# Stage 3 units one step earlier, the second set at step 14, and denser weight units

## The chip, the cores and the metric

The kernel runs on one core of a Trainium2 chip. A core has a matrix engine (TensorE, PE in the profile, with its weight loads as PEld), a vector engine (VectorE, DVE), an engine for activations (ScalarE, ACT), a general engine (GpSimd, POOL) and a queue engine (SyncE, SP), which here only issues DMAs. Each engine runs its own instructions in program order and waits on semaphores for the others. The metric is the device time of one execution in microseconds, as the median of several runs.

## The reference

Two layers. The first is a long convolution by FFT over a sequence of 12480 positions, for 4 batches and 128 channels, whose filter comes from a small MLP; the second is a feed-forward network with a gated activation.

```python
h_filt = (np.maximum(pos_emb @ w1, 0.0) @ w2) * np.exp(-0.01 * pos)[:, None]
u = x * v
L = 2 * S
y = irfft(rfft(u, n=L, axis=1) * rfft(h_filt, n=L, axis=0), n=L, axis=1)[:, :S, :]
t = (x * y).reshape(B * S, D)          # 49920 tokens of 128 channels
h = t @ w_in                           # 128 -> 2048
g = h * (1.0 / (1.0 + np.exp(-1.702 * h)))
out = g @ w_out                        # 2048 -> 128
```

## The kernel before

The FFT is done as matrix products in three stages. Stage 1 transforms along 120 positions (26 units, one per pair of residues), stage 2 transforms along the 52 residues, multiplies the spectra and transforms back (31 units), and stage 3 transforms back along the 120 positions and multiplies by x. Between the stages the data goes through DRAM (`g_d`, then `z_d`). The sequence is cut into five sets (`SETS`: block of the sequence, batch, number of batches), and each set passes all three stages. The result of stage 3 is cut into 104 halves of 480 tokens; sets 0 and 1 give 13 halves each, sets 2 to 4 give 26 each.

**The opening.** The loop from line 678 runs set 0 through stages 1 and 2, one tick per unit: `pipe.tick(u)` advances every live unit by one piece (a unit is a generator and each `yield` ends a piece; `yield 1` only splits a piece), so that up to seven units overlap. After each tick `heat` puts matmuls on a zero tile into the PE queue, and `wpipe.tick` advances the weight units: the FFN weights come in as 64-bit floats, and each of the eight weight units (`weight_unit`, line 543) turns a quarter of one weight matrix into a high and a low part by twelve DVE instructions on 128x512 elements and one on ACT. `WHEN` (line 40) lists the ticks at which a unit begins; its first piece is the DMA, and two ticks later its arithmetic begins, in pieces of two DVE instructions. Stage 1 units begin at ticks 0 to 25, stage 2 units at ticks 31 to 61. The last 24 spectra of stage 2 (`KEEP`) stay in a pool on chip, `keep`.

**The handover.** Seven ticks from line 703 run stage 3 for half 0. After that comes the main loop (line 714): for each half `n` eight steps `k`, each with one `mm1` (six matmuls of 480 columns into a PSUM pair `h`, then two activations, `gh` and `gf`), the `lo` of the step before (`gl`, the rest that `gh` leaves, on DVE), and the `mm2` of three steps before (six matmuls into `acc`). `mm1` of half `n` reads `xh` and `xl` of its stage 3 unit. In step 1 and step 9 the kept spectra are stored to DRAM on POOL's queue; in step `HOLD` the pool `keep` is closed, the rows of `z_d` that no unit writes are filled with zeros on the same queue, and the pool `main` is opened in its place. A tile of `main` waits until what lay there has been read.

**The feed.** From step `HOLD` on, `feed.run(1.0)` puts one step's share of the convolution of sets 1 to 4 behind the FFN matmuls of the step. `conv_feed` gives the units with weights and a mark for each set; `feed.pace` sets the rate so that the mark is reached in a given number of steps, and `feed.reach` puts in what is left. `when(n)` is the step in which the stage 3 unit of half `n` begins, `begin` the list of these for the first half of each set.

**Stage 3** (`p3_unit`, line 484): four DMAs (`zt` twice, `vt`, `x3`) on POOL's queue, or SP's for the first two halves; three ticks later sixteen matmuls into a PSUM bank (line 520), `yq` on ACT and two adds on DVE; a tick later the product with x (line 536), a tick later `xh` on ACT, a tick later `xl` on DVE (line 541). In the kernel before, the unit of half `n + 1` begins in step 0 of half `n`. So its matmuls stand in step 3, its `xl` in step 6, and `mm1` reads it eight steps after its beginning. There are three buffers of `xh` and `xl`, two each of `zt`, `vt` and `x3`. The PSUM pool of these banks holds three, shared with the feed.

The output of a half is copied out of `acc` with the last `mm2` and stored in step 4 of the next half, on POOL's queue.

Of the kernel before, what the change touches and what calls it, by code (L numbers as in the profile page):

```python
# [28 lines left out]
NP = N2 // 2  # L29
# [6 lines left out]
STEPS = FC // 2  # L36
KEEP = 24
AHEAD = 2
HOLD = 11
WHEN = (2, 7, 12, 17, 22, 38, 45, 52)  # L40

PAIRS = [(n, N2 - n) for n in range(1, NP)] + [(0, NP)]
SETS = [(0, 0, 1), (0, 1, 1), (0, 2, 2), (1, 0, 2), (1, 2, 2)]
# [12 lines left out]
NH = len(HV)  # L56
# [59 lines left out]
def conv_ffn_kernel(  # L116
# [22 lines left out]
    def pool(name, bufs, **kw):  # L139
        return ctx.enter_context(tc.tile_pool(name=name, bufs=bufs, **kw))  # L140
# [24 lines left out]
    def sb(name, shape, dt, bufs, tag=None, where="s"):  # L165
        return ps[where].tile(shape, dt, tag=tag or name, bufs=bufs, name=name)

    def bank():
        return ps["p"].tile([128, 512], F32, tag="cv", name="cv")
# [373 lines left out]
    def weight_unit(src, dst, s, rw):  # L543
        ts, stt = nc.vector.tensor_scalar, nc.vector.scalar_tensor_tensor
        raw = sb("raw", [128, WCH, 2], U32, 2)
        nc.sync.dma_start(out=raw.rearrange(rw[0], **rw[1]), in_=src)
        yield
        yield
        lo, hi = raw[:, :, 0], raw[:, :, 1]
        r, b, e = (sb(f"w{i}", [128, WCH], U32, 1) for i in range(3))  # L550
        t, q = (sb(f"w{i}", [128, WCH], F32, 1) for i in range(3, 5))
        ts(out=r, in0=lo, scalar1=29, scalar2=None, op0=ALU.logical_shift_right)
        stt(out=b, in0=hi, scalar=3, in1=r, op0=ALU.logical_shift_left, op1=ALU.bitwise_or)
        yield
        ts(out=b, in0=b, scalar1=0x7FFFFFFF, scalar2=0x40000000, op0=ALU.bitwise_and, op1=ALU.bitwise_xor)
        stt(out=b, in0=hi, scalar=0x80000000, in1=b, op0=ALU.bitwise_and, op1=ALU.bitwise_or)
        yield
        ts(out=e, in0=hi, scalar1=20, scalar2=0x7FF, op0=ALU.logical_shift_right, op1=ALU.bitwise_and)
        stt(out=t, in0=e, scalar=897, in1=b.bitcast(F32), op0=ALU.is_ge, op1=ALU.mult)
        yield  # L560
        w_hi = dst[0][:, s]
        act(w_hi, t, ACTF.Copy)
        ts(out=r, in0=lo, scalar1=6, scalar2=0x7FFFFF, op0=ALU.logical_shift_right, op1=ALU.bitwise_and)
        ts(out=b, in0=t.bitcast(U32), scalar1=0xFF800000, scalar2=None, op0=ALU.bitwise_and)
        yield
        tt(out=r, in0=r, in1=b, op=ALU.bitwise_or)
        tt(out=q, in0=r.bitcast(F32), in1=b.bitcast(F32), op=ALU.subtract)
        yield
        tt(out=t, in0=t, in1=w_hi.bitcast(F32), op=ALU.subtract)
        stt(out=dst[1][:, s], in0=q, scalar=2.0 ** -23, in1=t, op0=ALU.mult, op1=ALU.add)  # L570

# [71 lines left out]
    def fill(o, q):  # L643
        d = z_d[o][:, KZ:KP].rearrange("r k (q c) -> r (k q) c", c=128)
        q.dma_start(out=d, in_=zero.unsqueeze(1).broadcast_to([128, d.shape[1], 128]))

    with tc.manual_schedule():
        keep_cm = tc.tile_pool(name="keep", bufs=1, side="right", reuse_waits="tile")
        with tc.tile_pool(name="ps0", bufs=3, space=PSUM) as ps0, tc.tile_pool(name="ps0b", bufs=1, space=PSUM) as ps0b, \
                tc.tile_pool(name="st", bufs=1) as st:  # L650
            p1_cm = tc.tile_pool(name="p1", bufs=1, side="right")
            ps["s"], ps["p1"] = st, p1_cm.__enter__()
            ps["p"] = type("P", (), {"tile": staticmethod(
                lambda shape, dt, tag, name: (ps0 if tag == "cv2" else ps0b).tile(shape, dt, tag=tag, name=name))})
            nc.vector.memset(zero, 0.0)
            nc.vector.memset(w1_sb, 0.0)
            nc.vector.memset(w2_sb, 0.0)
            nc.vector.memset(sgn_sb[0:64], 1.0)
            nc.vector.memset(sgn_sb[64:128], -1.0)
            p1_load(0)  # L660
            for h in range(2):
                nc.sync.dma_start(out=w1_sb[64 * h:64 * h + 64, 64 * h:64 * h + 64], in_=w1)
                nc.sync.dma_start(out=w2_sb[64 * h:64 * h + 64, h], in_=w2)
            nc.sync.dma_start(out=win_sb, in_=c_win)
            wb = ps0b.tile([128, 512], F32, tag="wb", name="wb")

            def heat(k):
                for _ in range(2 * k):
                    mm(out=wb[:, 0:256], lhsT=warm[:, 0:128], rhs=warm, start=True, stop=True)

            heat(32)
            pipe, wpipe = Pipe(), Pipe()
            wu = list(weight_units())
            for c in range(1, AHEAD):
                p1_load(c)
            units = [p1_start(p) for p in range(NP)] + [None] * 5
            units += [p2_start(v) for v in range(NV)] + [None] * 9
            for n, u in enumerate(units):
                if n == NP + 9:
                    p1_cm.__exit__(None, None, None)  # L680
                    ps["k"] = keep_cm.__enter__()
                pipe.tick(u)
                heat(1 if 4 < n < NP else 6 if NP < n < NP + 6 else 2)
                if n == 4:
                    nc.sync.dma_start(out=wf, in_=c_wf)
                    nc.sync.dma_start(out=wv, in_=c_wi)
                    fill(0, nc.sync)
                wpipe.tick(wu.pop(0) if n in WHEN else None)
            assert not wu and not wpipe.live and not pipe.live
            heat(36)  # L690
        ps["f"] = pool("ffn", 1, reuse_waits="tile")
        ps["p"] = pool("ps1", 3, space=PSUM, reuse_waits="tile")
        ps["h"] = pool("ps2", 2, space=PSUM)
        p3 = Pipe()

        def when(n):
            return (n - 1) * STEPS

        first = {next(i for i, hv in enumerate(HV) if hv[0] == o): o for o in range(1, 5)}
        begin = sorted(when(n) for n in first)  # L700
        feed = Feed(pipe, *conv_feed())
        feed.pace(0, begin[0] - HOLD)
        for n in range(7):
            p3.tick(p3_unit(0) if n == 0 else None)
            if n == 1:
                act(sgn0, zero[:, 0:1], ACTF.Gelu_apprx_sigmoid)
            if n == 3:
                b = bank()
                for _ in range(20):
                    mm(out=b[:, 0:256], lhsT=warm[:, 0:128], rhs=warm, start=True, stop=True)  # L710
        gate = shared["a3"]
        ffn = Ffn()
        pend = []
        for n in range(NH):
            for k in range(STEPS):
                if pend:
                    ffn.lo(pend[-1])
                if len(pend) == LAG - 1 and pend[0][1] == STEPS - 1:
                    ffn.mm2(pend.pop(0))
                pend.append(ffn.mm1(n, k))  # L720
                t = n * STEPS + k
                if t == 1:
                    nc.gpsimd.tensor_tensor(out=sgn0, in0=gate[:, 0:1], in1=gate[:, 0:1], op=ALU.mult)
                if t == 1 or t == 9:
                    for _ in range(KEEP // 2):
                        spec_store(*spectra.pop(0), nc.gpsimd)
                if t == HOLD:
                    keep_cm.__exit__(None, None, None)
                    for o in range(1, 5):
                        fill(o, nc.gpsimd)  # L730
                    ps["s"] = ctx.enter_context(tc.tile_pool(name="main", bufs=1, side="right", reuse_waits="tile"))
                if len(pend) == LAG:
                    ffn.mm2(pend.pop(0))
                if t >= HOLD:
                    feed.run(1.0)
                if n + 1 < NH:
                    new = None
                    if k == 0:
                        if n + 1 in first:
                            o = first[n + 1]  # L740
                            feed.reach()
                            if o < 4:
                                feed.pace(o, begin[o] - begin[o - 1] - 2)
                            else:
                                feed.rate = 0.0
                        new = p3_unit(n + 1)
                    p3.tick(new)
                if k == 4:
                    ffn.store()
        ffn.lo(pend[-1])  # L750
        for it in pend:
            ffn.mm2(it)
        ffn.store()
# [123 lines left out]
```

## Time and profile before

| what | us |
|---|---|
| median of 3 runs (lowest, highest) | 3096.07 (3087.53, 3098.12) |
| the profiled execution | 3093.0 |
| its span, first to last instruction | 3091.2 |
| PE, DVE, ACT, POOL busy in the span | 2991.3, 2150.2, 2085.6, 470.6 |
| first stage 2 matmul | at 107.5 |
| first matmul of the FFN | at 210.5 |

The profile is of one execution. A view of waits names the engine and line that waited, what ended the wait, the total, the count and the longest. A view of groups or of a timeline names line, engine, operation, the tile written and the tiles read; "x4" is a count. A view of stretches gives, for each, its length, the busy time of PE, PEld, DVE, ACT and POOL with their instruction counts, the granted clock of PE (1.00 is full), the mean busy share of the 16 DMA engines, and GB/s. Matmul ends are modelled, so neighbouring matmuls overlap a little in such sums.

### The profile page before, as it was taken

The numbers are of one execution on the slowest core, as the hardware profiler recorded it, in microseconds if no ns is written. First come the engines' busy times: TensorE is split into PE (matmuls) and PEld (weight loads), VectorE is DVE, ScalarE is ACT, GpSimd is POOL, SyncE is SP. The second block draws the span as 40 slices with busy tenths as digits, with TensorE's granted clock in tenths as the row PEclk, the third lists the DMA queues.
The fourth block names the chain that finished last, engine by engine and source line by source line (L and its number), as shares of the span: only waits on it lengthen the run. The fifth ranks groups of instructions, "written<-read, shape, count | busy, mean of one in ns | idle before, by whom it ended". The sixth has DMA issues, their size and how long they took to land.

```text
span 3091.2 us, 42465 instructions
## 1 busy us (share of the span) xinstructions
PE 2991.3 (97%) x15478; PEld 2351.4 (76%) x15478; DVE 2150.2 (70%) x2909; ACT 2085.6 (67%) x2689; POOL 470.6 (15%) x765
## 2 busy tenths in 40 slices
PE   8898999999999999999999999999999999999999
PEld 4357876688766688777778887777778888888888
DVE  6555677777777766999996558888895445444454
ACT  3455776688777677666667766666666777677676
POOL 1353111012100111101111111111111111111110
PEclk9898999999999999999999999999999999999999
DMA  9878998999777976655565425455442111111110
GB/s 283 275 267 260 259 281 268 287 307 310 252 251 243 279 203 209 194 185 189 190 193 153 135 64 164 155 171 168 155 159 69 47 59 46 45 60 45 58 46 27
DMA packets 261105, 541.88 MB, mean 175 GB/s; under 512 B 30978, under 2 KB 120762, under 8 KB 260898
## 3 DMA queue, kind: packets, MB, share of 16 engines
q1 hardware_dynamic: 205970, 377.29, 38.4%
q0 software_dynamic: 54928, 161.86, 17.5%
q8 instruction: 125, 2.05, 0.3%
q14 instruction: 82, 0.67, 0.1%
HBM read 330.24 MB, written 208.80 MB: 174 GB/s over the span
## 4 chain that ended last, share of the span: by engine, by line
issue 38%; PE 17%; DVE 7%; POOL 4%; DMA 1%; ACT 0%; SPq 0%; POOLq 0%; DVEq 0%
PE h L595 7%; PE acc L612 7%; DVE fgl L603 2%; POOL zt L494 2%; DVE t L423 1%; PE cv L520 1%; POOL out_dram L623 1%; POOL x L500 1%; DVE t L439 1%; DVE t L438 1%; POOL vt L498 1%; DVE t L443 1%; PE ab L330 1%; DVE t L441 1%; PE cv L178 1%
## 5 line engine op out<-in xcount | busy, mean ns | idle before, releaser
L603 DVE TENSOR_TENSOR fgl<-fg,fgh 128x960 fp32r<-128x960 f32 x832 | 956.6, 1153 | 496.5 <-ACT fg L597 494.3
L596 ACT ACTIVATE fgh<-h 128x960 fp32r<-128x960 f32 x832 | 810.1, 974 | 548.5 <-PE h L595 547.7
L595 PE MATMUL h<-xh,wi 128*128 128x480 f32 x3328 | 1143.7, 388 | 9.2 <-ACT fg L597 8.4
L612 PE MATMUL acc<-fgh,wo 128*128 128x480 f32 x3328 | 871.9, 384 | 0.0
L597 ACT ACTIVATE fg<-h 128x960 f32<-128x960 f32 x832 | 805.9, 969 | 20.5 <-DVE fgl L603 20.0
L595 PEld LDWEIGHTS h<-xh,wi 128*128 128x128 f32 x3328 | 630.5, 189 | 184.7 <-issue 38.1
L612 PEld LDWEIGHTS acc<-fgh,wo 128*128 128x128 f32 x3328 | 629.6, 190 | 111.6 <-issue 12.2
L595 PE MATMUL h<-xl,wi 128*128 128x480 f32 x1664 | 638.2, 384 | 36.3 <-DVE xl L541 36.3
L612 PE MATMUL acc<-fgl,wo 128*128 128x480 f32 x1664 | 503.2, 384 | 0.5 <-DVE fgl L603 0.4
L595 PEld LDWEIGHTS h<-xl,wi 128*128 128x128 f32 x1664 | 315.0, 189 | 91.7 <-DVE xl L541 47.2
L623 POOL DMA_DIRECT2D out_dram<-ot x104 | 57.1, 549 | 1990.4 <-ACT ot L616 1990.2
L612 PEld LDWEIGHTS acc<-fgl,wo 128*128 128x128 f32 x1664 | 314.8, 189 | 51.7 <-DVE fgl L603 1.3
L520 PEld LDWEIGHTS cv<-vt,zt 122*128 122x128 f32 x1664 | 200.4, 192 | 26.2 <-issue 10.1
L520 PE MATMUL cv<-vt,zt 122*128 122x120 f32 x1664 | 204.8, 276 | 5.5 <-DMA vt<-in_c_v_dram 5.5
L324 PE MATMUL cv<-g,wf 52*64 52x512 f32 (+1 forms) x1240 | 174.4, 606 | 13.3 <-DMA g<-g_d 7.3
L494 POOL DMA_DIRECT2D zt<-z_d x204 | 148.4, 733 | 18.0 <-issue 6.5
L530 DVE TENSOR_TENSOR a<-cv,yq 128x240 f32<-128x240 f32 (+1 forms) x101 | 40.6, 402 | 139.9 <-ACT yq L528 139.9
L473 ACT ACTIVATE z<-ab 128x1024 f32<-128x1024 f32 (+2 forms) x124 | 112.6, 908 | 33.8 <-PE ab L330 28.6
L311 ACT ACTIVATE a<-cv 128x512 f32<-128x512 f32 x208 | 121.0, 602 | 17.3 <-PE cv L180 11.7
L459 DVE TENSOR_TENSOR t<-us,e 128x512 f32<-128x512 f32 (+2 forms) x62 | 58.5, 943 | 100.3 <-PE ab L330 55.6
L278 POOL DMA_DIRECT2D ft<-in_c_f_dram x108 | 57.5, 534 | 450.2 <-PE cv L180 436.4
L330 PE MATMUL ab<-t,wv 52*64 52x512 f32 (+2 forms) x992 | 120.3, 555 | 0.8 <-ACT fg L597 0.6
(90 smaller groups left out, 2559.6 us busy)
## 6 DMA issues: line engine op xcount, KB each, us to landing
g_d<-a SPq DMA_DIRECT2D x260, 256.0 KB
g<-g_d SPq DMA_DIRECT2D x300, 208.0 KB
zt<-z_d POOLq DMA_DIRECT2D x204, 256.0 KB, 4.9
e<-e_d SPq DMA_DIRECT2D x180, 256.0 KB
z_d<-z SPq DMA_DIRECT2D x90, 512.0 KB
xt<-in_xv_dram SPq DMA_DIRECT2D x78, 480.0 KB
u<-us_d SPq DMA_DIRECT2D x60, 512.0 KB
ft<-in_c_f_dram POOLq DMA_DIRECT2D x108, 240.0 KB, 4.7
```

The costliest lines, as they stand in the source:

```text
L311: act(a[:, ri], b, ACTF.Copy)
L324: mm(out=xy[q ^ c][64 * c:64 * c + 64, 0:256 * nw].rearrange("p (w c) -> p w c", w=nw), lhsT=wf[64 * q:64 * q + N2, c], rhs=g[64 * q:64 * ...
L330: mm(out=ab[h][64 * pl:64 * pl + 64, 0:w].rearrange("p (w c) -> p w c", w=nw), lhsT=wv[64 * h:64 * h + N2, pl], rhs=y[pl ^ h][64 * h:64 * ...
L473: act(zv.rearrange("p w a c -> p a w c"), ab[:, :, 0:wd].rearrange("p a (w c) -> p a w c", w=nw), ACTF.Copy)
L494: q.dma_start(out=zv[:, gq], in_=z_d[o][64 * gq + 2 * p0:64 * gq + 2 * p0 + 2 * npr].rearrange("r k c -> k r c"))
L520: mm(out=b[:, c0:c0 + M], lhsT=lhs, rhs=rhs, start=(k == 0), stop=(k == 1))
L595: mm(out=h[:, i, 0:TW], lhsT=wt[:, s], rhs=xx, start=st, stop=sp)
L596: act(gh, h[:, :, 0:TW], ACTF.Gelu_apprx_sigmoid)
L597: act(gf, h[:, :, 0:TW], ACTF.Gelu_apprx_sigmoid)
L603: tt(out=gl, in0=gf, in1=gh.bitcast(F32), op=ALU.subtract)
L612: mm(out=acc, lhsT=wt[:, 2 * k + i, :], rhs=xx[:, i], start=(t == 0 and i == 0 and k == 0), stop=(t == 2 and i == 1 and k == STEPS - 1))
L623: nc.gpsimd.dma_start(out=out[:, n], in_=ot)
```

## The change

- `when(n)` is one step less, and a stage 3 unit begins in the last step of the half before the half ahead of its own: the unit of half `n + 2` in step 7 of half `n`. The unit of half 1 begins in the last of the seven handover ticks, so that its DMAs stand on SP's queue where they stood, ahead of the main loop.
- `HOLD` is 14 instead of 11: the pool change, the zero fills and the feed begin three steps later, and the first mark has 95 - 14 = 81 steps instead of 96 - 11 = 85.
- `WHEN`: seven weight units begin at ticks 1 to 25, four ticks apart, and one at tick 47; before, five began at ticks 2 to 22, five apart, and three at 38, 45 and 52. Three `yield`s leave the weight unit, so that its arithmetic has three pieces of four DVE instructions.
- In ticks 27 to 31 `heat` is 9 instead of 6, so 18 matmuls on the zero tile instead of 12 in each.

```diff
--- before.py
+++ after.py
@@ -36,8 +36,8 @@
 STEPS = FC // 2
 KEEP = 24
 AHEAD = 2
-HOLD = 11
-WHEN = (2, 7, 12, 17, 22, 38, 45, 52)
+HOLD = 14
+WHEN = (1, 5, 9, 13, 17, 21, 25, 47)
 
 PAIRS = [(n, N2 - n) for n in range(1, NP)] + [(0, NP)]
 SETS = [(0, 0, 1), (0, 1, 1), (0, 2, 2), (1, 0, 2), (1, 2, 2)]
@@ -551,13 +551,11 @@
         t, q = (sb(f"w{i}", [128, WCH], F32, 1) for i in range(3, 5))
         ts(out=r, in0=lo, scalar1=29, scalar2=None, op0=ALU.logical_shift_right)
         stt(out=b, in0=hi, scalar=3, in1=r, op0=ALU.logical_shift_left, op1=ALU.bitwise_or)
-        yield
         ts(out=b, in0=b, scalar1=0x7FFFFFFF, scalar2=0x40000000, op0=ALU.bitwise_and, op1=ALU.bitwise_xor)
         stt(out=b, in0=hi, scalar=0x80000000, in1=b, op0=ALU.bitwise_and, op1=ALU.bitwise_or)
         yield
         ts(out=e, in0=hi, scalar1=20, scalar2=0x7FF, op0=ALU.logical_shift_right, op1=ALU.bitwise_and)
         stt(out=t, in0=e, scalar=897, in1=b.bitcast(F32), op0=ALU.is_ge, op1=ALU.mult)
-        yield
         w_hi = dst[0][:, s]
         act(w_hi, t, ACTF.Copy)
         ts(out=r, in0=lo, scalar1=6, scalar2=0x7FFFFF, op0=ALU.logical_shift_right, op1=ALU.bitwise_and)
@@ -565,7 +563,6 @@
         yield
         tt(out=r, in0=r, in1=b, op=ALU.bitwise_or)
         tt(out=q, in0=r.bitcast(F32), in1=b.bitcast(F32), op=ALU.subtract)
-        yield
         tt(out=t, in0=t, in1=w_hi.bitcast(F32), op=ALU.subtract)
         stt(out=dst[1][:, s], in0=q, scalar=2.0 ** -23, in1=t, op0=ALU.mult, op1=ALU.add)
 
@@ -680,7 +677,7 @@
                     p1_cm.__exit__(None, None, None)
                     ps["k"] = keep_cm.__enter__()
                 pipe.tick(u)
-                heat(1 if 4 < n < NP else 6 if NP < n < NP + 6 else 2)
+                heat(1 if 4 < n < NP else 9 if NP < n < NP + 6 else 2)
                 if n == 4:
                     nc.sync.dma_start(out=wf, in_=c_wf)
                     nc.sync.dma_start(out=wv, in_=c_wi)
@@ -694,14 +691,14 @@
         p3 = Pipe()
 
         def when(n):
-            return (n - 1) * STEPS
+            return (n - 1) * STEPS - 1
 
         first = {next(i for i, hv in enumerate(HV) if hv[0] == o): o for o in range(1, 5)}
         begin = sorted(when(n) for n in first)
         feed = Feed(pipe, *conv_feed())
         feed.pace(0, begin[0] - HOLD)
         for n in range(7):
-            p3.tick(p3_unit(0) if n == 0 else None)
+            p3.tick(p3_unit(n // 6) if n in (0, 6) else None)
             if n == 1:
                 act(sgn0, zero[:, 0:1], ACTF.Gelu_apprx_sigmoid)
             if n == 3:
@@ -733,18 +730,17 @@
                     ffn.mm2(pend.pop(0))
                 if t >= HOLD:
                     feed.run(1.0)
-                if n + 1 < NH:
-                    new = None
-                    if k == 0:
-                        if n + 1 in first:
-                            o = first[n + 1]
-                            feed.reach()
-                            if o < 4:
-                                feed.pace(o, begin[o] - begin[o - 1] - 2)
-                            else:
-                                feed.rate = 0.0
-                        new = p3_unit(n + 1)
-                    p3.tick(new)
+                new = None
+                if k == STEPS - 1 and n + 2 < NH:
+                    if n + 2 in first:
+                        o = first[n + 2]
+                        feed.reach()
+                        if o < 4:
+                            feed.pace(o, begin[o] - begin[o - 1] - 2)
+                        else:
+                            feed.rate = 0.0
+                    new = p3_unit(n + 2)
+                p3.tick(new)
                 if k == 4:
                     ffn.store()
         ffn.lo(pend[-1])
```

## The prediction

> **What bounds the kernel now.** The page comes first, for the span and the share of each engine.
>
> ```profile
> span 3091.2 us, 42465 instructions
> PE 2991.3 (97%) x15478; PEld 2351.4 (76%) x15478; DVE 2150.2 (70%) x2909; ACT 2085.6 (67%) x2689; POOL 470.6 (15%) x765
> ```
>
> PE (TensorE) is busy in 97% of the span, so a change that adds and removes no needed matmul can win only PE's 100 us of idle time and the time in which its clock is low. The second view is therefore PE's own waits; the columns are total us, times, longest us.
>
> ```profile
> PE h L595 <- DVE xl L541: 36.3, 29, 3.2
> ...
> PE cv L198 <- DMA pt<-in_posm_dram: 10.9, 2, 7.7
> ...
> PE cv L520 <- DMA vt<-in_c_v_dram: 5.5, 4, 3.8
> ```
>
> The largest is the first matmul of a half waiting for `xl`, the last product of the stage 3 unit of that half. The second row is two waits only, where the second set starts. The third view is those waits by stretch (from 240 to 1240, to 1660, to the end), then the busy time in the same stretches (us, PE, PEld, DVE, ACT, POOL, clock, DMA share, GB/s).
>
> ```profile
> PE h L595 <- DVE xl L541: 11.4, 9, 3.2
> PE h L595 <- DVE xl L541: 15.5, 12, 2.2
> PE h L595 <- DVE xl L541: 9.2, 7, 3.2
> ```
>
> ```profile
> 240.00:1240.00 1000.00, 960.61 (x4975) 741.65 (x4974) 707.24 (x1082) 725.85 (x1042) 155.92 (x263) 0.98 0.85 261
> 1240.00:1660.00 420.00, 401.99 (x2109) 304.50 (x2108) 401.41 (x542) 267.88 (x315) 46.07 (x76) 0.99 0.59 187
> 1660.00:3092.00 1432.00, 1416.01 (x7129) 1188.65 (x7127) 899.10 (x1029) 982.52 (x1166) 178.36 (x293) 1.00 0.30 95
> ```
>
> Three regimes: before 1240 DVE is 71% busy and the waits are bursts; from 1240 to 1660 DVE is 96% busy, as full as PE; after 1660 PE is nearly alone (99% busy, DVE 63%).
>
> **The change part by part.**
>
> *Stage 3 one step earlier.* No instruction is added; loads, `cv` matmuls, `a`, `xh` and `xl` of every unit move one FFN step up in program order. `xl` stood at the end of step 6 of a half and is needed at the head of the next half, one whole step later. Now it stands at the end of step 5. The length of a step is the distance of two first matmuls of neighbouring steps where nothing else runs:
>
> ```profile
> 2600.48 0.38 PE L595 MATMUL h<-xh,wi 128*128 128x480 f32 x1
> ...
> 2603.11 0.38 PE L595 MATMUL h<-xh,wi 128*128 128x480 f32 x1
> ```
>
> 2.63 us, more with convolution work in the step. The longest `xl` wait is 3.2 us, so one more step of lead covers nearly every single wait. Outside the saturated stretch (11.4 + 9.2 = 20.6 us) I count 18 us as gone; DVE has 29% and 37% of slack there to catch up. In the saturated stretch a wait that goes only lets PE run ahead until the next wait for DVE. What can be won there is the one extra step of lead, once, and the idle time that DVE owes to PE, which is this:
>
> ```profile
> DVE t L438 <- PE cv L324: 7.3, 10, 1.6
> ```
>
> It is DVE starved by a PE that had just waited: 7.3 us, plus about 3 us of lead, bounds the gain at 10; I take 8 of 15.5. Together 26 us, with ends at 11 (half of the unsaturated part alone) and 34. Next late behind `xl` would be `fgl` for the second matmul group, which is issued one step after its `h` and read three steps after: over two steps of lead. The `cv` matmuls move too, from step 3 to step 2, where PE has the second group of the half before and its own first group; their 1.94 us are neither more nor less. The moved loads stand on POOL's queue between the same two output stores as before, so they go out as early as they did; they are used one step sooner, and I cost that at nothing, the four waits for `vt` (5.5 us) staying.
>
> *The clock.* After long gaps the profile shows the granted clock at half for some us:
>
> ```profile
> 996.00:999.40 3.40, 3.40 (x12) 2.86 (x11) 0.12 (x1) 1.26 (x2) 0.00 (x0) 0.59 0.66 233
> 1037.00:1040.40 3.40, 3.40 (x11) 2.76 (x10) 3.37 (x6) 1.32 (x2) 0.00 (x0) 0.59 0.58 152
> 1853.00:1856.40 3.40, 3.40 (x12) 2.88 (x11) 3.40 (x6) 1.84 (x2) 0.00 (x0) 0.63 0.03 3
> ```
>
> Each of these three follows an `xl` wait of 2.4 to 3.2 us and loses 3.4 x 0.4 to 3.4 x 0.5, about 1.5 us; I count 5 us for the three, none to 9 as ends (in the saturated stretch DVE sets the pace anyway). The Trainium skill, "TensorE: Matmul & The Clock Gate", section "What's actually happening", says that the clock is halved only after an idle window of about 3.4 us. By that rule no `xl` wait costs clock, and the sum would be 5 us less of a gain; the three rows above speak against it.
>
> *The second set at step 14.* These rows of PE, SP's queue and POOL show the start of the second set (start us, us, ..., idle before and its releaser):
>
> ```profile
> 252.16 1.17 PE L198 MATMUL cv<-pt,w_sb 128*128 128x240 f32 x2 [3.17 <-DMA pt<-in_posm_dram]
> 269.37 1.17 PE L198 MATMUL cv<-pt,w_sb 128*128 128x240 f32 x2 [7.71 <-DMA pt<-in_posm_dram]
> 248.08 0.34 SPq L193 DMA_DIRECT2D pt<-in_posm_dram  x1
> 251.09 1.75 SPq L193 DMA_DIRECT2D pt<-in_posm_dram  x1
> 247.68 3.88 POOL L645 DMA_DIRECT2D z_d<-zero  x4
> 252.00:258.00 6.00, 5.84 (x15) 4.91 (x16) 0.00 (x0) 2.69 (x4) 2.62 (x6) 0.50 1.02 298
> ```
>
> Neither queue waits for a step: SP issues the first `pt` when the spectra that lay in its memory have been stored (248), POOL issues the zero fills right behind the last store. So `pt` still lands at 252 and 269 whatever the step. But PE has three more FFN steps to do before it asks: 252.16 - 3.17 = 249.0, and 249.0 + 3 x 2.63 = 256.9. The first wait goes, with the half clock behind it; the second shrinks: two more steps and about 1.3 us of small matmuls bring PE there at 263.5, so 269.4 - 263.5 = 5.9 of 7.7 are left. At 269.4 PE has then done three steps more than before, with the same convolution work: 7.9 us. I take 7, since the loads for the next stage 3 unit, now used one step earlier behind the same crowded DMA, may hold PE a little longer. Ends: 0, and 14 (both waits and half of a 6 us half-clock stretch). The convolution of set 2 then runs in 81 steps where it had 85, 5% denser; from 260 to 400 that meets a DVE 67% busy and a DMA share of 0.88, so it costs nothing, unless the DMA is full.
>
> ```profile
> 260.00:400.00 140.00, 132.29 (x612) 110.91 (x611) 93.19 (x174) 99.60 (x157) 26.02 (x46) 0.96 0.88 245
> ```
>
> *Stages 1 and 2.* Two weight units move from stage 2 into stage 1, each in three lumps of four DVE instructions where it had six of two. First the weight instructions alone (DVE, ACT), from 36 to 99 and from 107 to 206, then all engines, then rows of PE's timeline: ten stage 1 ticks, the heating and gap ahead of stage 2, three stage 2 ticks beside the first half of a weight unit and three beside the rest, and the first FFN matmul.
>
> ```profile
> 36.00:99.00 63.00, 33.42 (x52) 2.49 (x4) 1.00 0.92 294
> 107.00:206.00 99.00, 25.97 (x36) 1.90 (x3) 0.88 0.85 279
> 30.00:99.00 69.00, 61.34 (x218) 31.99 (x217) 56.46 (x120) 28.94 (x38) 14.49 (x20) 1.00 0.93 296
> 107.00:119.00 12.00, 11.48 (x47) 3.01 (x48) 3.86 (x6) 3.26 (x6) 2.81 (x4) 0.57 0.90 259
> 35.23 0.60 PE L206 MATMUL cv<-w_sb,rt 128*120 128x256 f32 x2
> 66.41 0.60 PE L206 MATMUL cv<-w_sb,rt 128*120 128x256 f32 x2
> 100.73 4.53 PE L669 MATMUL wb<-zero 128*128 128x256 bf16 x40
> 107.52 3.02 PE L324 MATMUL cv<-g,wf 52*64 52x512 f32 x8 [2.26 <-issue]
> 138.67 1.03 PE L324 MATMUL cv<-g,wf 52*64 52x512 f32 x8
> 144.64 1.09 PE L324 MATMUL cv<-g,wf 52*64 52x512 f32 x8
> 153.35 1.68 PE L324 MATMUL cv<-g,wf 52*64 52x512 f32 x8 [0.68 <-DMA g<-g_d]
> 210.55 0.48 PE L595 MATMUL h<-xh,wi 128*128 128x480 f32 x1 [0.47 <-ACT xh L539]
> ```
>
> A weight instruction takes 33.42/52 = 0.64 us in stage 1, so a unit takes 7.7 us and a lump 2.6. A stage 1 tick is (66.41 - 35.23)/10 = 3.1 us and its other DVE work about (56.46 - 33.42)/23 = 1.0 us. In five ticks that was 12.7 of 15.6 us; in four it is 11.7 of 12.5: DVE comes close to the tick, and three ticks of four hold 3.6 us of DVE work, the fourth only 1.0. A lumped tick can be 0.5 us too long; PE gets some of it back in the light one, so I take 0.2 us per tick over 24 ticks, 5 us (ends 0 and 15: 0.5 x 18 lumps is 9, and some half clock). In stage 2 a unit is 25.97/3 = 8.7 us of DVE. Its first three ticks take 2.0 us each (138.67 to 144.64), the other three 2.9 (to 153.35): a unit costs 2.7 us, and three cost 8. One unit remains, in lumps of 2.9, and costs about 4.5: a gain of 3.5, with 0 as its end since the DMA share there is 0.85. The 30 more heating matmuls (4.53/40 = 0.11 us each, 3.4 us) fill the 2.3 us gap ahead of stage 2 and may lift the 0.57 clock; 12 of them stand ahead of the last stage 1 matmuls and push them by 1.3 us. I count these as even, between 3 lost and 5 won. Stages 1 and 2: 1.5 us lost (from 8 won to 18 lost).
>
> **The sum**, against the profiled execution (3093.0 us, of it 3091.2 span; the median shown is 3096.07): 3093.0 - 26 - 5 - 7 + 1.5 = 3056.5; I say 3056.
>
> **The rivals.**
>
> 1. *The wait moves on.* PE, a step further ahead, meets the next DVE result: the lead is won once per stretch, not per half. For it: DVE at 96% from 1240 to 1660. Against it: 71% and 63% elsewhere. The `xl` gain is then 8 and the clock 1: 3056 + 18 + 4 = 3078.
> 2. *Step 14 wins nothing*, since the loads, not the step, end the wait, and another wait for the same DMA takes its place. For it: both queues ungated, DMA share 1.02. Against it: three steps of independent work. 3063.
> 3. *Stage 1 becomes DVE's.* All 18 lumps exposed, and the half clock after some: 15 to 20 us more, 3074.
> 4. *The clock is not freed*, by the page's rule above or because shorter waits suffice: 3061.
> 5. *Slower: L520 takes a bank.* In the halves in which DVE is late (29, by the count of `xl` waits), L520 now asks a step sooner for one of three PSUM banks that DVE has not emptied, and PE stands behind it, in order. It decides where DVE is more than a step late at step 2. At the longest wait of the saturated stretch, 2.2 us, 29 x 2.2 = 64 us: 3120. Against it: PE shows no wait of L520 for DVE now, though DVE is late there.
>
> **How the numbers follow.** Chances: forecast 0.46; rivals 0.17, 0.15, 0.13, 0.04, 0.05. The range 3036 to 3084 takes in rivals 1 to 4 and the favourable ends (34 of `xl`, 12 at step 14, 9 of clock); beyond it are the fifth and the tails of the first and third, and some luck below, under 0.2. About 0.3% (3087 to 3105) is what a measurement of this kernel can tell from no change. Faster: 0.46 + 0.15 + 0.04 and three quarters of 0.30, 0.87; within: the rest of the first and third, 0.08; slower: the fifth, 0.05.
>
> **What would show it.** `xl` waits of PE under 10 us in all, and hardly any before 1240 or after 1660; no half clock near 996, 1037 and 1853; one `pt` wait, of 4 to 7 us; the first `h` matmul at 210.5 + 1.5 = 212, within 8; `vt` waits no larger. It would be wrong if waits for `fgl`, `cv` banks or `vt` grow by what `xl` loses, or if the first `h` comes after 222.

## The result and the profile after

| | before | after | ratio, 95% interval |
|---|---|---|---|
| median, first comparison | 3095.32 us | 3053.35 us (3049.43 to 3060.53) | 0.9871 [0.9845, 0.9897] |
| median, beside its parts on another chip | 3091.38 us | 3055.41 us (3053.87 to 3062.74) | 0.9886 [0.9869, 0.9902] |
| profiled execution, its span | 3093.0, 3091.2 | 3054.41, 3052.6 | |

The change makes the kernel 1.1 to 1.3% faster; 3056 was forecast, in a range of 3036 to 3084. In the tables below the medians are of all runs, and the ratios leave out two slow executions, one of `heat_nine` (3246.94 us, granted clock 0.85) and one of the kernel before (9241.89 us). In the profile of the changed kernel the FFN lines stand three lower than before (L595 is L592, L597 is L594, L603 is L600, L612 is L609, L616 is L613). First PE's own waits in the changed kernel, in the columns of before (total us, times, longest):

```profile
PE h L592 <- ACT fg L594: 11.9, 11, 3.9
PE cv L198 <- DVE u L208: 9.6, 12, 1.1
PE cv L520 <- DMA vt<-in_c_v_dram: 6.5, 4, 4.0
PE cv L324 <- DMA g<-g_d: 6.1, 9, 2.0
PE cv L324 <- DVE t L361: 5.3, 4, 2.6
PE acc L609 <- DVE fgl L600: 5.2, 5, 1.7
...
PE cv L198 <- DMA pt<-in_posm_dram: 2.5, 1, 2.5
PE h L592 <- DVE xl L541: 2.0, 6, 0.6
```

The wait for `xl` was 36.3 us in 29 pieces and is 2.0 in 6. The `pt` waits were two, 10.9 us; one of 2.5 is left. Of the waits of the FFN matmuls two others have grown: for `fg` from 8.4 to 11.9, and for `fgl`, from 0.4 to 5.2. So some 8 of the 34 us came back under the names of the two results that ACT and DVE must deliver next. How much that is in time is read from the course of the execution: the copies of finished halves on ACT are marks that stand at the same place of the program in both kernels. From the timeline of ACT, before (L616) and after (L613), the marks of halves 16, 28 and 45 (the halves are numbered from 0):

```profile
803.50 0.57 ACT L616 ACTIVATE ot<-acc 128x480 f32<-128x480 f32 x1 [0.37 <-PE acc L612]
1196.63 0.57 ACT L616 ACTIVATE ot<-acc 128x480 f32<-128x480 f32 x1 [0.21 <-PE acc L612]
1687.22 0.57 ACT L616 ACTIVATE ot<-acc 128x480 f32<-128x480 f32 x1 [0.70 <-PE acc L612]
```

```profile
798.26 0.57 ACT L613 ACTIVATE ot<-acc 128x480 f32<-128x480 f32 x1 [0.31 <-PE acc L609]
1179.85 0.57 ACT L613 ACTIVATE ot<-acc 128x480 f32<-128x480 f32 x1 [0.81 <-PE acc L609]
1659.58 0.57 ACT L613 ACTIVATE ot<-acc 128x480 f32<-128x480 f32 x1 [0.18 <-PE acc L609]
```

The differences of such marks give the ledger of the change, in us (profiled executions; "FFN start" is the first `h` matmul):

| stretch | before | after | gain | forecast there |
|---|---|---|---|---|
| start to FFN start | 210.6 | 211.7 | -1.2 | -1.5 |
| FFN start to half 12 | 463.9 | 455.4 | 8.5 | 7, step 14 |
| half 12 to 16 | 129.1 | 131.1 | -2.0 | |
| half 16 to 28 | 393.1 | 381.6 | 11.5 | about 13, `xl` and clock |
| half 28 to 45, DVE saturated | 490.6 | 479.7 | 10.9 | 8, `xl` |
| half 45 to 103 | 1398.6 | 1387.9 | 10.7 | 9.5, `xl` and clock |

How the forecast falls on these stretches was worked out afterwards, from the prediction's rows; each row that has a term is within 3 us of it. The marks do not cut the convolution at quite the same place in both kernels: as a set now starts a step earlier, 16 matmuls of stage 2 stand ahead of half 16 instead of behind it (about 2 us: eight take 1.09 at full clock), and 3 of stage 1 ahead of half 12, and of half 45, instead of behind (some 0.7 us, an estimate from 0.23 for one).

The stretches view says what the gains are made of. Each pair of rows is the kernel before and the changed kernel, from half 16 to 28 and from half 28 to 45 (us, PE, PEld, DVE, ACT, POOL, clock, DMA share, GB/s):

```profile
803.50:1196.63 393.13, 374.52 (x1955) 280.47 (x1954) 275.63 (x354) 286.96 (x384) 51.95 (x87) 0.98 0.78 243
798.26:1179.85 381.59, 370.26 (x1939) 279.90 (x1938) 274.77 (x354) 286.14 (x381) 51.94 (x87) 0.98 0.81 251
```

```profile
1196.63:1687.22 490.59, 472.58 (x2458) 363.70 (x2457) 451.34 (x614) 319.51 (x383) 56.92 (x94) 0.99 0.60 189
1179.85:1659.58 479.73, 467.81 (x2461) 360.67 (x2460) 451.84 (x617) 319.83 (x384) 57.50 (x95) 1.00 0.61 191
```

PE's idle time is the length less its busy time. From half 16 to 28 it falls from 18.6 to 11.3 us, from half 28 to 45 from 18.0 to 11.9, and from half 45 on from 9.8 to 2.4: 20.8 us in all. The rest of the gain is busy time, and from half 28 to 45 that is the clock. Before, it stood at half three times in that stretch, each time from about the end of a wait for `xl` of 2.0 to 2.2 us; one of these waits, and the three pieces of half clock:

```profile
1359.96 0.49 PE L595 MATMUL h<-xl,wi 128*128 128x480 f32 x1 [2.03 <-DVE xl L541]
1360.70:1364.00 3.30, 3.30 (x10) 2.68 (x10) 3.27 (x5) 1.83 (x2) 0.00 (x0) 0.50 0.80 202
1418.70:1422.00 3.30, 3.16 (x8) 2.68 (x9) 3.30 (x5) 0.75 (x1) 0.00 (x0) 0.50 0.77 304
1565.50:1568.80 3.30, 3.30 (x10) 2.74 (x9) 3.27 (x5) 1.72 (x2) 0.00 (x0) 0.50 0.88 272
```

In the changed kernel there is none from half 28 to half 103. From half 16 to 28 the clock won nothing: in both kernels it stands at half for 13.7 us in all. The pieces near 996 and 1037 are gone, and in their place it stands at half behind a wait for `g` of 1.98 us and one for `fg` of 3.86; the third of these rows follows a wait for `vt` of 4.04, as one near 1091 did before.

```profile
1003.40:1006.70 3.30, 3.30 (x11) 2.62 (x9) 2.51 (x4) 1.46 (x4) 0.00 (x0) 0.50 1.02 344
1020.50:1023.80 3.30, 3.30 (x12) 2.19 (x14) 2.69 (x6) 1.96 (x3) 0.00 (x0) 0.50 0.85 271
1068.30:1075.00 6.70, 6.02 (x23) 5.63 (x24) 1.84 (x4) 0.37 (x1) 0.00 (x0) 0.50 0.63 193
```

DVE has the same work in both kernels from half 28 to 45, 451 to 452 us, and its share of that stretch rises from 92% to 94%. A last row bears on the heating:

```profile
107.00:119.00 12.00, 11.35 (x75) 4.55 (x72) 2.64 (x5) 3.26 (x6) 2.82 (x4) 1.00 0.86 243
```

At the head of stage 2 the clock is 1.00 where it was 0.57 in the profile of the kernel before. Over all profiles: in the 12 us from the first stage 2 matmul it stands at half for 0 to 10.2 us, 4.7 on average, in the eight with the opening of before, and for 0.6 us at most in the five with the new one.

### The profile page after: what moved, and what is told of

Its sections match the earlier page's. It is cut to its first block, busy times and chain, and to the rows that moved or that the text cites. A ratio compares the mean times of both kernels' runs of the same rounds, so it can differ in the third digit from the quotient of the medians.

```text
span 3052.6 us, 42552 instructions
## 1 busy us (share of the span) xinstructions
PE 2983.5 (98%) x15508; PEld 2349.7 (77%) x15508; DVE 2148.7 (70%) x2909; ACT 2091.3 (69%) x2689; POOL 466.7 (15%) x765
## 4 chain that ended last, share of the span: by engine, by line
PE 57%; DVE 7%; issue 1%; DMA 1%; ACT 0%; SPq 0%; POOL 0%; DVEq 0%; POOLq 0%
PE h L592 24%; PE acc L609 24%; PE cv L520 4%; DVE fgl L600 2%; PE ab L330 1%; DVE t L423 1%; PE cv L324 1%; DVE t L438 1%; DVE t L439 1%; DVE t L443 1%; PE cv L178 1%; PE cv L180 1%; PE cv L179 1%; DVE t L441 0%; DMA u<-us_d 0%
## 5 line engine op out<-in xcount | busy, mean ns | idle before, releaser
L600 DVE TENSOR_TENSOR fgl<-fg,fgh 128x960 fp32r<-128x960 f32 x832 | 956.9, 1154 | 426.0 <-ACT fg L594 424.3
L592 PE MATMUL h<-xh,wi 128*128 128x480 f32 x3328 | 1149.4, 386 | 12.6 <-ACT fg L594 11.9
L609 PE MATMUL acc<-fgh,wo 128*128 128x480 f32 x3328 | 866.4, 382 | 0.0
L594 ACT ACTIVATE fg<-h 128x960 f32<-128x960 f32 x832 | 804.3, 967 | 65.3 <-DVE fgl L600 65.0
L592 PEld LDWEIGHTS h<-xh,wi 128*128 128x128 f32 x3328 | 628.0, 189 | 188.6 <-ACT fg L594 37.8
L609 PEld LDWEIGHTS acc<-fgh,wo 128*128 128x128 f32 x3328 | 625.8, 188 | 110.9 <-issue 12.9
L592 PE MATMUL h<-xl,wi 128*128 128x480 f32 x1664 | 634.3, 381 | 2.0 <-DVE xl L541 2.0
L609 PE MATMUL acc<-fgl,wo 128*128 128x480 f32 x1664 | 502.5, 383 | 5.2 <-DVE fgl L600 5.2
L609 PEld LDWEIGHTS acc<-fgl,wo 128*128 128x128 f32 x1664 | 312.6, 188 | 57.4 <-DVE fgl L600 7.8
L592 PEld LDWEIGHTS h<-xl,wi 128*128 128x128 f32 x1664 | 313.8, 189 | 50.2 <-DVE xl L541 5.0
L520 PEld LDWEIGHTS cv<-vt,zt 122*128 122x128 f32 x1664 | 203.1, 194 | 28.9 <-issue 16.8
L520 PE MATMUL cv<-vt,zt 122*128 122x120 f32 x1664 | 207.6, 279 | 8.3 <-DMA vt<-in_c_v_dram 6.5
```

The source lines that it names most:

```text
L520: mm(out=b[:, c0:c0 + M], lhsT=lhs, rhs=rhs, start=(k == 0), stop=(k == 1))
L592: mm(out=h[:, i, 0:TW], lhsT=wt[:, s], rhs=xx, start=st, stop=sp)
L594: act(gf, h[:, :, 0:TW], ACTF.Gelu_apprx_sigmoid)
L600: tt(out=gl, in0=gf, in1=gh.bitcast(F32), op=ALU.subtract)
L609: mm(out=acc, lhsT=wt[:, 2 * k + i, :], rhs=xx[:, i], start=(t == 0 and i == 0 and k == 0), stop=(t == 2 and i == 1 and k == STEPS - 1))
```

## The experiments

The waits and the ledger fit the theory of the prediction, but they are those of three edits together. So each was run alone on the kernel before, then taken out of the changed kernel, and the lead itself was varied. Ratios are to the kernel before, run beside each kernel on the same chip (its medians were 3087.6 to 3091.4 in the three comparisons).

### Each part alone

*The stage 3 step alone* (`st3_only`): the edits of `when`, of the seven handover ticks and of the start of `p3_unit` in the main loop, with `HOLD`, `WHEN`, the lumps and the heat of before.

> The kernel before with the stage 3 units alone one step earlier. If the step of lead of xl is what counts: 3062 to 3068, PE's xl waits under 5 us in all, the half clocks at 996, 1037 and 1853 gone, the start of the FFN and of the second set as before (first h at 210.5, pt waits 3.2 and 7.7). If the gain came from the handover and the opening: within 10 us of before. If the wait only moves on in the saturated stretch: no more than 8 us gained between the halves that end near 1240 and 1660.

*Step 14 alone* (`hold_only`):

```diff
-HOLD = 11
+HOLD = 14
```

> The kernel before with the second set at step 14 alone. If the loads land when they did and PE merely has three more steps to do: 3086 to 3090, the first pt wait gone, the second 3 to 6 us, and the end of half 12 (673 us before) about 8 us earlier. If another wait for the same DMA takes the place: half 12 ends within 2 us of before.

*The opening alone* (`open_only`): `WHEN`, the three `yield`s and `heat` of the change.

> The kernel before with the weight units and the heating of the opening alone. Theory: what stage 1 loses and stage 2 wins are even, first h at 211 to 213, total within 3 us of before. Rival, the clock: the half clocks of the opening go and with them 5 us or more, first h under 207. Rival, DVE in stage 1: first h over 216.

| kernel | median us | ratio, 95% interval | FFN start to half 12 | half 12 to 103 |
|---|---|---|---|---|
| before | | 1 | 463.9 | 2411.4 |
| `st3_only` | 3059.73 | 0.9912 [0.9884, 0.9939] | 466.6 | 2379.4 |
| `hold_only` | 3091.73 | 1.0002 [0.9984, 1.0020] | 468.6 | 2412.5 |
| `open_only` | 3091.57 | 1.0016 [1.0003, 1.0029] | 461.2 | 2412.0 |
| changed kernel | 3053.35 | 0.9871 [0.9845, 0.9897] | 455.4 | 2380.3 |

The stage 3 step is the gain: everything that the changed kernel wins behind half 12 (31 us) it wins alone (32). PE's first wait in it is no longer `xl` but

```profile
PE h L595 <- ACT fg L597: 13.1, 12, 3.8
PE cv L198 <- DMA pt<-in_posm_dram: 12.5, 2, 9.3
```

and the three half clocks near 996, 1037 and 1853 are gone with it, though two stand near 1004 and 1021, behind other waits, as in the changed kernel. Step 14 alone gains nothing, against the expectation of 7, and the opening alone loses some 5 us by its ratio (1 to 9 by the interval). The three ratios multiply to 0.993, the changed kernel is at 0.987 to 0.989: that is the question of the next group.

### The lead of xl without the earlier loads

`late_loads` takes one piece out of `p3_unit` of the kernel before, so that matmuls, `xh` and `xl` come a step earlier and the loads do not.

```diff
         xts[n] = xh, xl
         yield
         yield
-        yield
         b = bank()
```

> The kernel before with one piece less between loads and matmuls of a stage 3 unit: loads in step 0 as before, matmuls in step 2, xl in step 5. If the place of xl alone decides: as st3_only, 3062 to 3068, but with vt waits at the set starts larger by up to a step each (5.5 us becomes 8 to 16). If the earlier loads are part of the gain: less than half of it, 3078 or more.

Measured: 3087.55 us, ratio 1.0003 [0.9989, 1.0016], so neither expectation: no gain at all. Its PE waits:

```profile
PE cv L519 <- DMA vt<-in_c_v_dram: 22.4, 8, 7.4
PE h L594 <- ACT fg L596: 13.8, 14, 3.4
PE cv L198 <- DMA pt<-in_posm_dram: 12.2, 2, 7.4
...
PE h L594 <- DVE xl L540: 2.3, 4, 1.2
```

The `xl` waits are gone as wholly as in the changed kernel, and from half 28 to the end it is nearly as fast (481.9 us from half 28 to 45, 1387.7 from there to half 103). What it lost stands before: `vt` waits of 0.8 to 7.4 us, seven of the eight before 1240, and from the start of the FFN to half 12 476.2 us, where the kernel before takes 463.9. The loads are thus part of the edit: with `xl` a step earlier and the loads where they were, the halves up to 28 give back what the rest wins. (The stage 3 step also ends each set's convolution a step sooner, which `late_loads` leaves as it was; the two were not tried apart.)

### Taken out of the changed kernel

`st3_hold` is the changed kernel with the opening of before, `hold_11` the changed kernel with `HOLD = 11`, `whole` the changed kernel itself, and `lead_two` has the units two steps earlier:

```diff
-                if k == STEPS - 1 and n + 2 < NH:
+                if k == STEPS - 2 and n + 2 < NH:
...
-            return (n - 1) * STEPS - 1
+            return (n - 1) * STEPS - 2
...
-            p3.tick(p3_unit(n // 6) if n in (0, 6) else None)
+            p3.tick(p3_unit(n // 5) if n in (0, 5) else None)
```

> The changed kernel again, beside its parts on one chip. The ratios of the three parts to before were 0.9912, 1.0002 and 1.0016; if they add up, this is 0.993, about 22 us faster than before on this chip. If step 14 pays only together with the earlier stage 3 units, it is 0.987, about 40 us faster, as first measured.

> The changed kernel with the opening of before (weight ticks, lumps and heat undone). If the opening costs what it showed alone (0.16%), this is 4 to 6 us faster than the whole. If the opening is even, as predicted, within 2 us of the whole.

> The changed kernel with the second set at step 11 again. If step 14 is worth 7 us beside the earlier stage 3 units, this is 5 to 9 us slower than the whole; if it is worth nothing, as it was alone, within 2 us of the whole, and the first stall of 3 us with its half clock is back but paid for elsewhere in set 1.

> The changed kernel with the stage 3 units two steps earlier than before in place of one. If one step of lead covers the waits and DVE or the buffers of fg limit the rest: within 4 us of the whole, xl waits of PE 0, the waits for fg and fgl (11.9 and 5.2) no smaller. If lead is still what is short: 5 to 10 us faster than the whole, all between the halves that end near 1240 and 1630.

| kernel | median us | ratio, 95% interval | FFN start to half 12 | half 28 to 45 |
|---|---|---|---|---|
| `whole` | 3055.41 | 0.9886 [0.9869, 0.9902] | 457.9 | 479.7 |
| `st3_hold` | 3050.05 | 0.9869 [0.9854, 0.9884] | 458.2 | 479.7 |
| `hold_11` | 3062.99 | 0.9914 [0.9897, 0.9931] | 467.6 | 480.1 |
| `lead_two` | 3057.16 | 0.9890 [0.9875, 0.9904] | 465.2 | 481.7 |

Step 14 is worth 7.6 us here by the medians (`whole` against `hold_11`; the two intervals just meet). In the profiles its gain stands between the start of the FFN and half 12 (457.9 against 467.6). The opening costs 5.4 by the medians (`whole` against `st3_hold`). A second step of lead gains nothing over all, and the saturated stretch is no shorter. This is a balance: behind half 12 `lead_two` takes 2373.2 us where the changed kernel takes 2380.3 and `whole` 2382.3, some 3 of these 7 to 9 us because a stage 3 unit and a few matmuls of the convolution have moved ahead of the mark; and ahead of half 12 it loses as much. There the second step of lead changes the wait of the second set; PE in `lead_two`:

```profile
PE h L592 <- ACT fg L594: 18.2, 20, 3.9
PE cv L520 <- DMA vt<-in_c_v_dram: 14.1, 2, 9.9
```

One of these two waits, 9.9 us, stands at 270, where `cv` now meets loads that are still on their way at the crowded start of set 1.

### Step 14 again, and two tries at more

`hold_again` and `st3_again` are `hold_only` and `st3_only` once more, with more runs. `heat_nine` is `st3_hold` with the more heat; `fg_three` is `st3_hold` with

```diff
-        xh, xl = (sb(nm, [128, TW], F32R, 3, where="f") for nm in ("xh", "xl"))
+        xh, xl = (sb(nm, [128, TW], F32R, 2, where="f") for nm in ("xh", "xl"))
...
-            gf = sb("fg", [128, 2, TW], F32, 2, where="f")
+            gf = sb("fg", [128, 2, TW], F32, 3, where="f")
```

> Step 14 alone once more, beside the stage 3 step alone. If it is worth nothing without the earlier stage 3 units: ratio to before 0.998 to 1.002, and half clocks between halves 4 and 12 as in its first profile. If the first measurement fell unluckily: 0.997 or less, 7 us or more.

> The stage 3 step alone once more. Predicted by its share of the forecast, 31 us: ratio 0.990. The first measurement was 0.9912 with an interval of 0.003; if it stands, step 14 adds 7 us or more beside it that it does not bring alone.

> The stage 3 step and step 14 with the opening of before, but with the more heat. The whole opening costs about 5 us. If it is the denser weight units: this is within 2 us of the same kernel without the heat (3050). If it is the heat, 12 matmuls ahead of the last stage 1 products: 3 to 6 us above it.

> The stage 3 step and step 14 with the opening of before, and a third buffer of fg (xh and xl have two instead of three to make room). In the changed kernel ACT waits 65 us for fgl to free a buffer of fg, and PE 12 us for ACT behind it. If these two buffers are the new limit: the waits of PE for fg fall under 4 us and the time is 5 to 10 us under 3050. If DVE's own work sets the pace of that stretch: PE's waits only change their name (fgl, xl), and the time is within 3 us of 3050.

| kernel | median us | ratio, 95% interval |
|---|---|---|
| `hold_again` | 3091.90 | 1.0006 [0.9997, 1.0015] |
| `st3_again` | 3060.74 | 0.9913 [0.9899, 0.9927] |
| `heat_nine` | 3049.84 | 0.9868 [0.9853, 0.9883] |
| `fg_three` | 3045.31 | 0.9860 [0.9845, 0.9874] |

Step 14 alone is nothing, now within 0.15%; beside the stage 3 step it is 0.9913 to 0.9869, 13 us with intervals that do not meet. Where it is given back shows in the ledger. The `pt` wait shrinks in both, and from half 0 to 4 both are ahead of before (162.7 us): 148.2 in `hold_again`, 152.1 in `st3_hold`. About 3 us of that is work put off, since the feed starts three steps later and some 20 matmuls of the convolution then stand behind half 4. From half 4 to 12 (273.7 before) `hold_again` takes 286.7, `hold_only` 291.2 and `st3_hold` 278.9. The stretch from half 4 to 12 and PE's waits in it, in the kernel before, in `hold_again` and in `st3_hold`:

```profile
400.76:674.41 273.65, 264.37 (x1495) 192.62 (x1494) 202.82 (x351) 193.12 (x296) 34.20 (x57) 0.99 0.92 284
385.90:672.60 286.70, 272.83 (x1516) 199.56 (x1515) 207.39 (x361) 196.49 (x304) 37.28 (x63) 0.97 0.91 280
386.90:665.81 278.91, 274.99 (x1523) 198.80 (x1522) 210.43 (x367) 198.19 (x304) 35.76 (x60) 0.99 0.95 291
```

```profile
PE h L595 <- ACT fg L597: 3.9, 5, 1.6
PE h L595 <- DVE xl L541: 2.2, 3, 0.7
PE cv L324 <- DMA g<-g_d: 2.1, 3, 1.0
PE cv L520 <- DMA vt<-in_c_v_dram: 1.1, 2, 0.6
```

```profile
PE cv L324 <- DMA g<-g_d: 4.4, 2, 3.5
PE h L595 <- DVE xl L541: 3.5, 3, 1.5
PE cv L520 <- DMA vt<-in_c_v_dram: 3.3, 2, 2.6
PE h L595 <- ACT fg L597: 2.0, 4, 0.9
```

```profile
PE cv L324 <- DMA g<-g_d: 2.0, 2, 1.7
PE cv L520 <- ACT uh L295: 1.0, 1, 1.0
PE cv L520 <- ACT fg L597: 0.5, 1, 0.5
PE h L595 <- ACT fg L597: 0.2, 1, 0.2
```

Against the kernel before, the 13 us that `hold_again` loses here are some 3 of work put off, 4.6 more of idle time (13.9 against 9.3) and some 6 of clock (an estimate: 0.02 of 287 us). The waits that have grown are those for the DMA, `g` and `vt`, from 3.2 to 7.7 us together; those for `xl` and `fg` have not, 6.1 and 5.5. With `xl` and the loads of stage 3 a step earlier, idle time is 3.9 us, the clock is back at 0.99, the waits for `xl` and `vt` are gone, and those for `fg` nearly. So the two edits help each other, and the rows show in which waits. Why `g` and `vt` come later in the one than in the other was not tried, and stays open.

`heat_nine` and `st3_hold` have the same ratio within 0.0001, so the denser weight units are the likelier cause of the 5 us that the opening loses. But each interval is 4.6 us wide to either side, so that a cost of the heat of a few us is not excluded, and the other profiles hint at one: from the last matmul of line 206 in stage 1 to the first matmul of stage 2, where the heating stands, the eight profiles with the old opening take 12.9 us on average, the five with the new one 14.2. And a third buffer of `fg` shortens nothing where it was meant to: the saturated stretch is 479.4 us beside 479.7. PE's waits between 1225 and 1625, in `st3_hold` and then in `fg_three`:

```profile
PE h L595 <- ACT fg L597: 6.9, 7, 1.6
PE acc L612 <- DVE fgl L603: 3.1, 3, 1.2
...
PE h L595 <- DVE xl L541: 0.7, 3, 0.2
```

```profile
PE acc L612 <- DVE fgl L603: 5.5, 4, 2.2
PE h L595 <- DVE xl L541: 3.2, 5, 1.1
PE h L595 <- ACT fg L597: 2.0, 2, 1.2
```

10.7 us under one set of names, 10.7 under another (11.9 and 11.3 with the row for `ab` in each). This fits DVE setting the pace of the stretch, as the expectation had it. It is not shown by this run alone, since the edit also took a buffer from `xl`, which may be why its waits grew. `fg_three` has the lowest ratio of all, but its interval overlaps that of `st3_hold` and that of `whole`, and it was not run side by side with either.

## Why the prediction was right, and where it was not

- **Stage 3 one step earlier, 26 us, and the clock, 5.** Right in sum, and right in its mechanism, the wait for `xl`. Alone the edit gave 27 us (0.9912), and behind half 12 31 to 32 us in the profiles; the 4 us between are lost up to half 12, where `st3_only` takes 466.6 us and the kernel before 463.9 or, in `open_only`, 461.2. The split between the two terms was less good. PE's idle time behind half 16 fell by 20.8 us where 26 were counted, some 2 of these ahead of it: 14.7 us outside the saturated stretch, against 18, and 6.1 inside, against 8. The clock gave somewhat more than its 5, and not where it was counted: of the three pieces named, the two near 996 and 1037 were replaced by others, and only the one near 1853 was won. But the three pieces of the saturated stretch went too, which the prediction put at nothing because DVE sets the pace there. At half for 10.2 us, they are worth about 5 us by themselves, an estimate, and PE's busy time in that stretch is 4.8 us less. So the 10.9 us gained there, against 8 forecast and a bound of 10, agree in part by luck: the waits alone stayed well inside the bound. The bound rested on DVE's 7.3 us of starvation and one step of lead; in the changed kernel that starvation is gone from the waits of DVE, and `lead_two` and `fg_three` point the same way: there more lead and more buffers changed only the names of the waits.
- **"I cost that at nothing"**, of loads used one step sooner. This holds for the edit as it was made, in which the loads move too: `vt` waits went from 5.5 to 6.5 us. `late_loads` shows what the step rested on: without the earlier loads the same lead of `xl` is worth nothing.
- **Step 14, 7 us.** Right for the change, as far as it can be measured (7.6 by the medians beside the rest, 8.5 in the ledger, 13 in the kernels with the opening of before), and by its mechanism: the first `pt` wait gone, the second 2.5 us, and 7.5 in the other profile, where 5.9 was worked out. The sentence that failed is that the denser convolution "costs nothing, unless the DMA is full". Alone, with the DMA at a share of 0.91 from half 4 to 12, step 14 loses there what it had won, 13 us and 17.5 in two profiles; it stays cheap only with the earlier stage 3 units. The rival that step 14 wins nothing was right about the kernel before, and in part by the way it gave: waits for the same DMA (`g` and `vt`, 4.5 us more) came in place of the `pt` waits, and lower clock with them.
- **Stages 1 and 2, 1.5 us lost.** The size was off: 5.4 by the medians, and in the eight profiles with the old opening the FFN starts at 206.6 us on average (201.5 to 210.6), in the five with the new one at 211.5 (208.3 to 215.6). The stage 1 term was right. In the changed kernel's PE timeline 16 ticks take 52.9 us, 3.30 each against 3.12, the 0.2 per tick that was forecast:

```profile
38.66 0.60 PE L206 MATMUL cv<-w_sb,rt 128*120 128x256 f32 x2
...
91.52 0.60 PE L206 MATMUL cv<-w_sb,rt 128*120 128x256 f32 x2
```

  The term that was mis-sized is the gain of 3.5 us in stage 2. From the start of its first matmul to the start of its last it took 87.1 us on average in the eight profiles with the old opening and 87.8 in the five with the new one, with two weight units fewer and a full clock at its head. Its mean clock is 0.93 in both, so what was won at the head was lost further on. Why it is not shorter was not tried: PE's idle time in it is less (9.3 us on average against 10.9), and the bound given, no gain because of the DMA, is where it came out.
- **The rivals.** The wait did move on in the saturated stretch, but only after 6.1 us of idle time and the clock had been won there, and outside it 14.7 us of idle time were won too, so the gain did not end at 8 over all. L520 did not stall for a bank that DVE held: no profile shows a PE wait of L520 for DVE, and those for ACT are at most 2.1 us in all. The half clocks that were lost with the `xl` waits speak against the fourth rival: from half 28 on, four pieces of half clock each stood behind an `xl` wait of 2.0 to 3.2 us, and all four went with these waits in the changed kernel. By the rule of the Trainium skill ("TensorE: Matmul & The Clock Gate", "What's actually happening") the clock is halved after an idle window of about 3.4 us. That rule does not bound the waits that matter here: in the kernel before, shorter ones, of 2.0 to 3.2 us, had half clock right behind them.

## What to carry to other kernels

Where an in-order engine is late only in bursts, a step more of lead removes its waits, and the gain can be read off beforehand stretch by stretch; where it is busy all the time, count the starved time and the lead once and no more, count the clock apart from the waits, and expect new names for the rest. Move the loads of a unit together with its compute: the same lead without them was worth nothing. And an edit whose effect alone is nothing can be worth its price beside another; test it both alone and by taking it out.

## What the runs showed of the hardware that was not expected

The opening is not reproducible to better than some us: with the same instructions ahead of it the first FFN matmul stood between 201.5 and 210.6 us in eight profiles, more spread than the edits of the opening were worth, while from half 28 to 45 the kernels with the stage 3 step and two buffers of `fg` agree within 0.5 us (479.6 to 480.1, six profiles).
